# Weight conversion with three VectorE operations a tile; low parts of 18 weight tiles and key sums of two batches made on GpSimd

## The chip, the cores and the metric

The kernel runs on one core of a Trainium2 chip, as one launch. The metric is the device time in microseconds (us) of that core. The core has five engines that run side by side, each through its own list of instructions in a fixed order: TensorE (PE in the profile; PEld is its weight load), VectorE (DVE), ScalarE (ACT), GpSimd (POOL) and SyncE (SP, which here only issues DMAs). An instruction that waits for another engine holds up all that stand behind it on its own engine.

## The reference

Three stages follow each other, each in float32:

```python
k_p = k.reshape(B, H, Sp, 8, D).mean(axis=3)      # 8 batches, 8 heads, 576 keys -> 72
v_p = v.reshape(B, H, Sp, 8, D).mean(axis=3)
attn = softmax(q @ k_p.T / sqrt(D))               # sums get + 1e-9
x = (attn @ v_p) as (4608 tokens, 512)
x = max(x @ w1, x @ w2, x @ w3) @ w_out           # 512 -> 768 -> 512
h = x @ w_in                                      # 512 -> 2048
out = (h - tanh(h)) @ w_out2                      # 2048 -> 512
```

The five weight matrices arrive as float64 and are turned into float32 on the chip, from their bits.

## The kernel before

Every matmul operand is split into a high part H (rounded to the PE's own 32-bit format) and a low part L (the rest), and a product is made of three matmuls: H·H, H·L and L·H.

**Attention (first third).** The tokens are cut into tiles of at most 128 (`tiles`) and these into units that end at a batch's end or at a block of 512 tokens. A key sum (`k_red`, L188) adds eight neighbours of one head pair: one VectorE reduction. `k_split` (L197 on ScalarE, L201 on VectorE) makes H and L of a batch's sums, the tile `kbd`. The value sums (`pool_sum`, L205 to L207) are three GpSimd additions that halve 8 to 4, 2 and 1. Per token tile follow scores (`qk`), maximum (L304), exponentials (L307 on ScalarE), division (L315 to L317), transposes (`tr`, L335, L346) with their splits (L337, L338, L348, L349). At a unit's end `av` (L356 to L359) multiplies with the values; its result is split into `xH` (L363, ScalarE) and `xL` (L364, VectorE), the input of the next stage. The first units have 512, 64 and 448 tokens with four such `xL` each: so the ninth `xL` in the order begins the third unit, which completes the second block.

**First MLP.** `moe_group` (L523 to L529) makes 12 matmuls for one weight tile i and one block j. 18 weight tiles are needed by each of 9 blocks. `moe_part` mixes groups with attention steps in an order written by hand: four groups of block 0 stand in front of the end of the third unit, all others behind it.

**Weight conversion (`Conv`).** A tile of 128x512 float64 is loaded as pairs of 32-bit words (`raw`, three buffers). ScalarE takes the magnitude of the upper word as if it were a float32 (`mag`, L94, into `ma`, four buffers). VectorE then clamps and scales it (L101), shifts it left by 3 (L103), puts in the sign (L105), and the upper three bits of the lower word (L107). For the first 18 tiles `split_to` then makes wH (L128, ScalarE) and wL (L129, VectorE). Another 32 tiles (the weights of the second MLP) go to DRAM and are split later (L602, L603), and six tiles (`wo1`) have their low part made on GpSimd.

**Second MLP (from about 767 us).** `h2`, `gact` and `prod`; results leave PSUM by L734 (ScalarE) or L736 (VectorE), those of the stage in between by L663 or L665.

The order of the instructions on each engine is set by a scheduler that goes through the program and may take a later instruction of an engine first, where it reckons that the earlier one would have to wait. Operations marked `keep_in_program_order` stay where they are. Buffers come free when their last reader is done.

Of the kernel before, what the change touches and what calls it, by code (L numbers as in the profile page):

```python
# [7 lines left out]
F32 = mybir.dt.float32  # L8
# [4 lines left out]
AF = mybir.ActivationFunctionType  # L13
ALU = mybir.AluOpType
# [18 lines left out]
NF = FF // 128  # L33
# [19 lines left out]
def moe_chain_kernel(ctx, tc, qt, kt, vm, vl, ident, cst, w123, wo1, win, wout, out):  # L53
    nc = tc.nc
    V, A, G, T, Q = nc.vector, nc.scalar, nc.gpsimd, nc.tensor, nc.sync
# [3 lines left out]
    def pool(name, bufs=1, side="left", **kw):  # L59
        cm = tc.tile_pool(name=name, bufs=bufs, side=side, **kw)  # L60
        stacks[name] = cm
        return cm.__enter__()
# [11 lines left out]
    srcs = [(win if c % 2 == 0 else wout)[c // 2] for c in range(2 * NC2)]  # L74
# [3 lines left out]
    class Conv:  # L78


        def __init__(self, st, srcs, done, pin=lambda i: i):
            self.st, self.srcs, self.done, self.n, self.pin = st, srcs, done, len(srcs), pin
            self.raw, self.a, self.i = {}, {}, 0

        def load(self, i):
            if i < self.n and i not in self.raw:
                t = self.st.tile([128, 512, 2], I32, tag="raw", name="raw", bufs=RAWS)
                Q.dma_start(out=t.bitcast(I64).rearrange("p n o -> p (n o)"), in_=self.srcs[i])
                self.raw[i] = t

        def mag(self, i):
            if i < self.n:
                a = self.st.tile([128, 512], I32, tag="ma", name="ma", bufs=4)
                self.pin(A.activation(a.bitcast(F32), self.raw[i][:, :, 1].bitcast(F32), AF.Abs))  # L94
                self.a[i] = a

        def bits(self, i):
            if i < self.n:
                raw, a = self.raw[i], self.a[i]
                lo, hi = raw[:, :, 0], raw[:, :, 1]  # L100
                self.pin(V.tensor_scalar(out=a.bitcast(F32), in0=a.bitcast(F32), scalar1=2.0 ** -15,  # L101
                                         scalar2=2.0 ** -80, op0=ALU.max, op1=ALU.mult))
                V.tensor_scalar(out=a, in0=a, scalar1=3, scalar2=0x7FFFFFFF,  # L103
                                op0=ALU.logical_shift_left, op1=ALU.bitwise_and)
                V.scalar_tensor_tensor(out=a, in0=hi, scalar=-2147483648, in1=a,  # L105
                                       op0=ALU.bitwise_and, op1=ALU.bitwise_or)
                V.scalar_tensor_tensor(out=a, in0=lo, scalar=29, in1=a,  # L107
                                       op0=ALU.logical_shift_right, op1=ALU.bitwise_or)

        def step(self):  # L110
            i = self.i
            if i > self.n:
                return
            if i == 0:
                for k in range(RAWS):
                    self.load(k)
                self.mag(0)
            if i > 0:
                self.done(i - 1, self.a.pop(i - 1).bitcast(F32))
            self.mag(i + 1)  # L120
            self.bits(i)
            self.load(i + RAWS)
            self.i += 1

    def split_to(outs, eng):
        def done(i, w):
            H, L = outs[i]
            A.copy(H, w)  # L128
            eng.tensor_tensor(out=L, in0=w, in1=H.bitcast(F32), op=ALU.subtract)  # L129
        return done  # L130
# [6 lines left out]
    sta = pool("sta")  # L137
# [9 lines left out]
    wH = [wa.tile([128, 4, 128], F32R, name=f"wH{i}") for i in range(18)]  # L147
    wL = [wa.tile([128, 4, 128], F32R, name=f"wL{i}") for i in range(18)]
# [29 lines left out]
    kraw, vraw, vxraw, ksum, vsum, vxsum = {}, {}, {}, {}, {}, {}  # L178
# [6 lines left out]
    def k_red(b, p):  # L185
        if b not in ksum:
            ksum[b] = at.tile([128, NP, SP], F32, tag="ksum", name="ksum")
        r = V.tensor_reduce(out=ksum[b][:, p, :], in_=kraw.pop((b, p)), axis=AX.X, op=ALU.add)  # L188
        if b > 1:
            tc.keep_in_program_order(r)  # L190
# [13 lines left out]
    def pool_sum(o, t):  # L204
        G.tensor_tensor(out=t[:, :, 0:4], in0=t[:, :, 0:4], in1=t[:, :, 4:8], op=ALU.add)  # L205
        G.tensor_tensor(out=t[:, :, 0:2], in0=t[:, :, 0:2], in1=t[:, :, 2:4], op=ALU.add)
        G.tensor_tensor(out=o, in0=t[:, :, 0], in1=t[:, :, 1], op=ALU.add)  # L207
# [209 lines left out]
    for n in range(ntl + 1):  # L417
        last = n == ntl
        if not last:
            b = tiles[n][0]  # L420
# [57 lines left out]
    for _ in range(NP - 1):  # L478
# [2 lines left out]
    q_load(2)  # L481
    Q.dma_start(out=consts, in_=cst)
    cv = Conv(sta, [w123[i] for i in range(18)],
              split_to([tuple(t[i].rearrange("p a b -> p (a b)") for t in (wH, wL)) for i in range(18)], V))
    cv.load(0)
    Q.dma_start(out=idt, in_=ident)
    next_v()
# [66 lines left out]
    def point(x):  # L554

        j = int(x)
        if j >= NA - 1:
# [6 lines left out]
    moe_part(gr(1)[:4], point(2.2))  # L564
    moe_part([g for p in zip(gr(0)[4:], gr(1)[4:]) for g in p], point(3), conv=lambda k: k % 2 == 0)
    cv = Conv(sta, srcs, lambda i, w: tc.keep_in_program_order(Q.dma_start(out=wsc[i], in_=w)),
              tc.keep_in_program_order)
    for i in range(RAWS):
        cv.load(i)
    for j in range(2, NA - 1):  # L570
# [6 lines left out]
    wo = pool("wo", side="right")  # L577
    woH = [wo.tile([128, 512], F32R, name=f"woH{i}") for i in range(NF)]
    woL = [wo.tile([128, 512], F32R, name=f"woL{i}") for i in range(NF)]
    cv = Conv(sta, [wo1[i] for i in range(NF)], split_to(list(zip(woH, woL)), G))  # L580
    for i in range(RAWS):
        cv.load(i)
    moe_part(gr(NA - 1), pos[0])
# [9 lines left out]
    def w_load():  # L593
        i = nw[0]
        if i < 2 * NC2:
            Q.dma_start(out=wt[i][1].bitcast(F32), in_=wsc[i])
            nw[0] += 1

    def w_split():
        i = nw[1]  # L600
        h, l = wt[i]
        A.copy(h, l.bitcast(F32))  # L602
        G.tensor_tensor(out=l, in0=l.bitcast(F32), in1=h.bitcast(F32), op=ALU.subtract)  # L603
        nw[1] += 1

    def load_split(src, eng):
        l = io.tile([128, 512], F32R, tag="L", name="ioL", bufs=8)
        r = l.bitcast(F32)
        Q.dma_start(out=r, in_=src)
        t = [None, l]  # L610

        def split():
            h = io.tile([128, 512], F32R, tag="H", name="ioH", bufs=7)
            A.copy(h, r)  # L614
            eng.tensor_tensor(out=l, in0=r, in1=h.bitcast(F32), op=ALU.subtract)  # L615
            t[0] = h

        return t, split

    def hsrc(j, kc):  # L620
        g, o = divmod(j * BB, HG)
        return hs[g][kc][:, o:o + BB]
# [5 lines left out]
    def c_load(eng):  # L628
        i = nld[0]
        if i < len(xl_):  # L630
            j, kc = xl_[i]
            ct[i] = load_split(xs[j][kc], eng)
            nld[0] += 1

    def c_split():
        i = nsp[0]
        if i < len(xl_):
            ct[i][1]()
            nsp[0] += 1
# [8 lines left out]
    for i, (j, kc) in enumerate(loads):  # L648
        if kc == 0:
            acc = [psm.tile([128, 512], F32, tag="mm", name="ps_mm") if j % 2 else  # L650
                   ps2.tile([128, 512], F32, tag="sc" if e < 2 else "tr", name="ps_acc") for e in range(NE)]
        (h, l), _ = lt.pop(i)
        if i + SPL < len(loads):
            lt[i + SPL][1]()
        for e in range(NE):
            c = slice(e * 128, e * 128 + 128)
            T.matmul(acc[e], woH[kc][:, c], h, start=(kc == 0), stop=False)  # L657
            T.matmul(acc[e], woH[kc][:, c], l, start=False, stop=False)  # L658
            T.matmul(acc[e], woL[kc][:, c], h, start=False, stop=(kc == NF - 1))  # L659
            if kc == NF - 1:  # L660
                ob = io.tile([128, 512], F32, tag="ob", name="ob", bufs=4)
                if e % 2 == 0:
                    A.copy(ob, acc[e])  # L663
                else:
                    V.tensor_copy(ob, acc[e])  # L665
                Q.dma_start(out=xs[j][e], in_=ob)
        if i + AHEAD < len(loads):
            lt[i + AHEAD] = load_split(hsrc(*loads[i + AHEAD]), V)
        else:
            c_load(V)  # L670
        if i >= len(loads) - 2:
            c_split()
            c_split()
        w_load()
        while nw[1] < min(2 * NC2, i * 2 * NC2 // (len(loads) - 4)):
            w_split()
# [43 lines left out]
    def prod(j, c):  # L720
        gH, gL = gs.pop((j, c))
        oh, ol = wt[2 * c + 1]
        for t in range(NE):
            r = slice(t * 128, t * 128 + 128)
            if c == 0:
                accs[j, t] = psc.tile([128, 512], F32, tag="acc", name="ps_acc", bufs=5)
            acc = accs[j, t]
            T.matmul(acc, gH[:, r], oh, start=(c == 0), stop=False)  # L728
            T.matmul(acc, gH[:, r], ol, start=False, stop=False)  # L729
            T.matmul(acc, gL[:, r], oh, start=False, stop=(c == NC2 - 1))  # L730
            if c == NC2 - 1:
                ob = io.tile([128, 512], F32, tag="ob", name="ob", bufs=4)
                if t % 2 == 0:
                    A.copy(ob, acc)  # L734
                else:
                    V.tensor_copy(ob, acc)  # L736
                r0 = j * BB + t * 128
                Q.dma_start(out=out[r0:r0 + 128, :], in_=ob)

# [72 lines left out]
```

## Time and profile before

| | us |
|---|---|
| three timed runs | 1550.59, 1552.76, 1554.56 |
| median | 1552.76 |
| profiled execution, from first to last instruction (span) | 1548.8 |
| median less span | 4.0 |
| PE, PEld busy | 1508.3, 1250.4 |
| DVE, ACT, POOL busy | 1154.0, 823.5, 195.5 |

A line of the profile names the line of the kernel, the engine, the operation, the output and inputs by their names in the program and the shapes (partitions x elements). "Idle before" is the time that the engine stood still just ahead of such instructions, and what ended it. Instructions of one engine overlap a little: on VectorE the next one begins some 0.08 us ahead of the recorded end. PEclk is the clock that PE was granted, as a share of full speed.

### The profile page before, as it was taken

How to read it: one execution, taken by the hardware profiler on the slowest of the kernel's cores; microseconds unless marked ns; L12 is line 12 of the kernel's file. 1: busy time of each engine (PE TensorE's matmuls, PEld its weight loads, DVE VectorE, ACT ScalarE, POOL GpSimd, SP SyncE). 2: the span in 40 equal slices, each digit the busy share in tenths (PEclk: the TensorE clock that was granted, in tenths of full speed). 3: DMA queues.
4: the chain of work that ended last, by engine and by line, in shares of the span. 5: the costliest groups of instructions: out<-in, count | busy, mean ns of one | idle time of the engine just before them, and what ended most of it. 6: DMA issues, size and time to landing. Idle time of an engine off the chain costs nothing.

```text
span 1548.8 us, 20108 instructions
## 1 busy us (share of the span) xinstructions
PE 1508.3 (97%) x6896; PEld 1250.4 (81%) x6896; DVE 1154.0 (75%) x2050; ACT 823.5 (53%) x2059; POOL 195.5 (13%) x223
## 2 busy tenths in 40 slices
PE   4899999999999999999999999999999999999999
PEld 4678878888888788888888888888888888888887
DVE  7998378777777831533488888888888888888886
ACT  7664266555566510632455555555555555555554
POOL 4503020202100110920001000010101000010000
PEclk9889999999999999999999999999999999999999
DMA  7645144545332511955300000010100000010000
GB/s 260 182 136 173 58 138 145 173 147 180 123 120 96 182 50 51 328 188 174 123 1 28 28 28 28 1 55 0 55 1 28 28 28 28 0 55 0 28 1 28
DMA packets 68614, 134.55 MB, mean 87 GB/s; under 512 B 11552, under 2 KB 11680, under 8 KB 68512
## 3 DMA queue, kind: packets, MB, share of 16 engines
q1 hardware_dynamic: 68512, 133.27, 26.5%
q8 instruction: 54, 0.88, 0.2%
q14 instruction: 48, 0.39, 0.1%
HBM read 91.82 MB, written 41.42 MB: 86 GB/s over the span
## 4 chain that ended last, share of the span: by engine, by line
PE 89%; DVE 8%; ACT 1%; issue 1%; DMA 0%; ACTq 0%; DVEq 0%; SPq 0%
PE ps_mm L715 8%; PE ps_mm L717 8%; PE ps_acc L730 8%; PE ps_acc L728 8%; PE ps_acc L729 8%; PE ps_mm L716 8%; PE ps_mm L523 8%; PE ps_mm L524 8%; PE ps_mm L525 8%; PE ps_acc L659 2%; PE ps_acc L658 2%; PE ps_acc L657 2%; PE ps_mm L659 1%; PE ps_mm L658 1%; PE ps_mm L657 1%; PE ps_sc L283 1%
## 5 line engine op out<-in xcount | busy, mean ns | idle before, releaser
L523 PE MATMUL ps_mm<-xH,wH 128*128 128x512 f32 x648 | 260.0, 402 | 0.0
L524 PE MATMUL ps_mm<-xL,wH 128*128 128x512 f32 x648 | 254.2, 392 | 0.0
L525 PE MATMUL ps_mm<-xH,wL 128*128 128x512 f32 x648 | 253.8, 392 | 0.0
L703 ACT CAST gH<-w 128x512 fp32r<-128x512 f32 x144 | 89.4, 621 | 301.3 <-DVE w L702 301.3
L715 PE MATMUL ps_mm<-ioH,ctH 128*128 128x512 f32 x576 | 224.2, 389 | 0.8 <-ACT ioH L614 0.8
L717 PE MATMUL ps_mm<-ioH,ctL 128*128 128x512 f32 x576 | 224.1, 389 | 0.0
L716 PE MATMUL ps_mm<-ioL,ctH 128*128 128x512 f32 x576 | 224.1, 389 | 0.0
L728 PE MATMUL ps_acc<-ctH,gH 128*128 128x512 f32 x576 | 224.1, 389 | 0.0
L729 PE MATMUL ps_acc<-ctL,gH 128*128 128x512 f32 x576 | 224.1, 389 | 0.0
L730 PE MATMUL ps_acc<-ctH,gL 128*128 128x512 f32 x576 | 224.1, 389 | 0.0
L704 DVE TENSOR_TENSOR gL<-w,gH 128x512 fp32r<-128x512 f32 x144 | 103.9, 722 | 92.1 <-ACT gH L703 86.5
L529 DVE TENSOR_TENSOR h<-h,ps_mm 128x512 f32<-128x512 f32 x108 | 73.9, 685 | 104.2 <-PE ps_mm L525 102.9
L525 PEld LDWEIGHTS ps_mm<-xH,wL 128*128 128x128 f32 x648 | 121.9, 188 | 25.9
L615 POOL TENSOR_TENSOR ioL<-ioL,ioH 128x512 fp32r<-128x512 f32 x32 | 49.3, 1558 | 728.9 <-ACT ioH L614 728.9
L523 PEld LDWEIGHTS ps_mm<-xH,wH 128*128 128x128 f32 x648 | 122.6, 189 | 22.7
L524 PEld LDWEIGHTS ps_mm<-xL,wH 128*128 128x128 f32 x648 | 122.4, 189 | 22.5 <-DVE xL L364 0.3
L715 PEld LDWEIGHTS ps_mm<-ioH,ctH 128*128 128x128 f32 x576 | 108.2, 188 | 23.7 <-ACT ioH L614 1.2
L729 PEld LDWEIGHTS ps_acc<-ctL,gH 128*128 128x128 f32 x576 | 108.1, 188 | 22.6
L717 PEld LDWEIGHTS ps_mm<-ioH,ctL 128*128 128x128 f32 x576 | 108.1, 188 | 22.5
L730 PEld LDWEIGHTS ps_acc<-ctH,gL 128*128 128x128 f32 x576 | 108.1, 188 | 22.4
L716 PEld LDWEIGHTS ps_mm<-ioL,ctH 128*128 128x128 f32 x576 | 108.1, 188 | 22.4
L728 PEld LDWEIGHTS ps_acc<-ctH,gH 128*128 128x128 f32 x576 | 108.0, 188 | 22.3
(106 smaller groups left out, 2843.9 us busy)
## 6 DMA issues: line engine op xcount, KB each, us to landing
hs<-h SPq DMA_DIRECT2D x54, 256.0 KB, 2.0
ioL<-hs SPq DMA_DIRECT2D x54, 256.0 KB, 3.2
kraw<-kt SPq DMA_DIRECT2D x32, 288.0 KB, 3.3
raw<-w SPq DMA_DIRECT2D x18, 512.0 KB, 3.8
xs<-ob SPq DMA_DIRECT2D x36, 256.0 KB, 2.1
ioL<-xs SPq DMA_DIRECT2D x36, 256.0 KB, 3.4
out<-ob SPq DMA_DIRECT2D x36, 256.0 KB, 2.2
qraw<-qt SPq DMA_DIRECT2D x32, 256.0 KB, 3.0
```

The costliest lines, as they stand in the source:

```text
L523: T.matmul(ps[:, :BA], wH[i][:, kc], xh[:, kc], start=(kc == 0), stop=False)
L524: T.matmul(ps[:, :BA], wH[i][:, kc], xl[:, kc], start=False, stop=False)
L525: T.matmul(ps[:, :BA], wL[i][:, kc], xh[:, kc], start=False, stop=(kc == NE - 1))
L529: V.tensor_tensor(out=t, in0=t, in1=ps[:, :BA], op=ALU.max)
L703: A.copy(gH, w)
L704: V.tensor_tensor(out=gL, in0=w, in1=gH.bitcast(F32), op=ALU.subtract)
L715: T.matmul(ps, wh[:, kc], xh, start=(kc == 0), stop=False)
L716: T.matmul(ps, wh[:, kc], xl2, start=False, stop=False)
L717: T.matmul(ps, wl_[:, kc], xh, start=False, stop=(kc == NE - 1))
L728: T.matmul(acc, gH[:, r], oh, start=(c == 0), stop=False)
L729: T.matmul(acc, gH[:, r], ol, start=False, stop=False)
L730: T.matmul(acc, gL[:, r], oh, start=False, stop=(c == NC2 - 1))
```

## The change

- `Conv` takes the engine for a new step `low`, which shifts the lower word right by 29 in place (VectorE in all three uses, one source and one result with a step of 8 bytes). The clamp, the scale and the separate shift go: the scale moves into the ScalarE magnitude, one operation shifts left and joins the low bits, one joins the sign. VectorE has three operations a tile (L94, L108 and L110 of the changed file) in place of four.
- The weights are now larger by 2 to the 8th. Results are scaled back where they leave PSUM, by 2 to the -24 and 2 to the -8.
- wL of the first 18 tiles is made on GpSimd.
- The key sums of the batches counted 1 and 2 (the second and third of eight) are made on GpSimd by `pool_sum`, three additions each.

```diff
@@ class Conv
+        def low(self, i):
+            if i < self.n:
+                lo = self.raw[i][:, :, 0]
+                self.pin(self.eng.tensor_scalar(out=lo, in0=lo, scalar1=29, scalar2=None,
+                                                op0=ALU.logical_shift_right))
...
-                self.pin(A.activation(a.bitcast(F32), self.raw[i][:, :, 1].bitcast(F32), AF.Abs))
+                self.pin(A.activation(a.bitcast(F32), self.raw[i][:, :, 1].bitcast(F32), AF.Abs,
+                                      scale=2.0 ** -111))
...
-                self.pin(V.tensor_scalar(out=a.bitcast(F32), in0=a.bitcast(F32), scalar1=2.0 ** -15,
-                                         scalar2=2.0 ** -80, op0=ALU.max, op1=ALU.mult))
-                V.tensor_scalar(out=a, in0=a, scalar1=3, scalar2=0x7FFFFFFF,
-                                op0=ALU.logical_shift_left, op1=ALU.bitwise_and)
+                self.pin(V.scalar_tensor_tensor(out=a, in0=a, scalar=3, in1=lo,
+                                                op0=ALU.logical_shift_left, op1=ALU.bitwise_or))
                 V.scalar_tensor_tensor(out=a, in0=hi, scalar=-2147483648, in1=a,
                                        op0=ALU.bitwise_and, op1=ALU.bitwise_or)
-                V.scalar_tensor_tensor(out=a, in0=lo, scalar=29, in1=a,
-                                       op0=ALU.logical_shift_right, op1=ALU.bitwise_or)
...
@@ def k_red
+        if b in (1, 2):
+            pool_sum(ksum[b][:, p, :], kraw.pop((b, p)))
+            return
...
-              split_to([tuple(t[i].rearrange("p a b -> p (a b)") for t in (wH, wL)) for i in range(18)], V))
+              split_to([tuple(t[i].rearrange("p a b -> p (a b)") for t in (wH, wL)) for i in range(18)], G), V)
...
-                    A.copy(ob, acc[e])
+                    A.activation(ob, acc[e], AF.Copy, scale=2.0 ** -24)
                 else:
-                    V.tensor_copy(ob, acc[e])
+                    V.tensor_scalar(out=ob, in0=acc[e], scalar1=2.0 ** -24, scalar2=None, op0=ALU.mult)
```

Behind the same change of the two lines that write `out` (2 to the -8) and the new arguments of the three `Conv` calls nothing else differs.

VectorE, end of the first batch, where the second batch's keys (`kbd_168`) are split. Before:

```order
L188 TENSOR_REDUCE ksum<-kraw 128x72 x2
L129 TENSOR_TENSOR wL_150<-ma,wH_132 128x512
L101 TENSOR_SCALAR ma<-ma 128x512 x2
L338 TENSOR_TENSOR eL<-ps_tr,eH 128x4x128
L349 TENSOR_TENSOR eX<-ps_tr,eX 32x2x128
L201 SCALAR_TENSOR_TENSOR kbd_168<-ksum,kbd_168 64x4x72 x2
```

The same place now:

```order
L312 TENSOR_REDUCE nb<-ps_sc 64x4 x2
L209 SCALAR_TENSOR_TENSOR kbd_168<-ksum,kbd_168 64x4x72
L346 TENSOR_TENSOR eL<-ps_tr,eH 128x4x128
L209 SCALAR_TENSOR_TENSOR kbd_168<-ksum,kbd_168 64x4x72
L108 SCALAR_TENSOR_TENSOR ma<-ma,raw 128x512
L110 SCALAR_TENSOR_TENSOR ma<-raw,ma 128x512
```

The key sums and wL_150 are gone from VectorE, and the first half of the split stands ahead of the fourth tile's `eL`.

ScalarE at the same place (L197 before and L205 now are the splits, L307 and L315 the exponentials, here of the fifth tile with 64 tokens). Before:

```order
L307 ACTIVATE sc,su<-ps_sc,nb 64x72 x4
L319 COPY lf<-sc 128x192
L307 ACTIVATE sc,su<-ps_sc,nb 64x72 x4
L337 CAST eH<-ps_tr 128x4x128
L348 CAST eX<-ps_tr 96x2x128
L197 ACTIVATE kbd_168<-ksum 64x4x72 x2
```

Now:

```order
L205 ACTIVATE kbd_168<-ksum 64x4x72 x2
L327 COPY lf<-sc 128x192
L100 ACTIVATE ma<-raw 128x512
L133 CAST wH_132<-ma 128x512
L345 CAST eH<-ps_tr 128x4x128
L315 ACTIVATE sc,su<-ps_sc,nb 64x72 x8
```

The split stands in front of the fifth tile's exponentials and of the fourth tile's `eH`, which it stood behind.

GpSimd from the last value sums of the first batch on. Before:

```order
L207 TENSOR_TENSOR vxsum<-vxraw 96x64
L205 TENSOR_TENSOR vraw<-vraw 128x64x4
L206 TENSOR_TENSOR vraw<-vraw 128x64x2
L207 TENSOR_TENSOR vsum<-vraw 128x64
L205 TENSOR_TENSOR vraw<-vraw 128x64x4
```

Now, from one row earlier in the program:

```order
L215 TENSOR_TENSOR vsum<-vraw 128x64
L134 TENSOR_TENSOR wL_149<-ma,wH_131 128x512
L213 TENSOR_TENSOR vxraw<-vxraw 96x64x4
...
L213 TENSOR_TENSOR vraw<-vraw 128x64x4
L214 TENSOR_TENSOR vraw<-vraw 128x64x2
L213 TENSOR_TENSOR kraw<-kraw 128x72x4
L214 TENSOR_TENSOR kraw<-kraw 128x72x2
L215 TENSOR_TENSOR ksum<-kraw 128x72
L213 TENSOR_TENSOR kraw<-kraw 128x72x4
```

A low part stands ahead of the first batch's last value sums, and the four key sums of the second batch follow the first steps of two value sums.

## Rows read from the trace of the kernel before

**Rows 1.** Busy time by stretch: us, then PE, PEld, DVE, ACT, POOL, PEclk.

```profile
10.00:40.00 30.00, 17.27 (x80) 15.30 (x79) 27.50 (x58) 25.82 (x112) 15.11 (x25) 1.00 0.78 260
40.00:86.00 46.00, 37.13 (x167) 29.32 (x167) 43.66 (x94) 32.54 (x132) 20.40 (x36) 0.82 0.56 165
86.00:140.00 54.00, 53.87 (x252) 45.09 (x252) 51.85 (x109) 30.01 (x91) 12.43 (x18) 0.97 0.56 176
```

**Rows 2.** Waits of PE from 10 to 86 us: total, times, longest.

```profile
PE ps_tr L335 <- DVE sc L317: 11.0, 6, 3.8
```

**Rows 3.** Groups by line on DVE from 10 to 86 us: count, busy us, mean ns.

```profile
L188 DVE TENSOR_REDUCE ksum<-kraw 128x72 f32<-128x576 f32 x9 | 6.6, 742 | 0.0
L105 DVE SCALAR_TENSOR_TENSOR ma<-raw,ma 128x512 int32<-128x512 int32 x7 | 5.7, 828 | 0.0
L103 DVE TENSOR_SCALAR ma<-ma 128x512 int32<-128x512 int32 x8 | 5.2, 679 | 0.0
L107 DVE SCALAR_TENSOR_TENSOR ma<-raw,ma 128x512 int32<-128x512 int32 x6 | 5.1, 845 | 0.0
```

**Rows 4.** Instructions of DVE in order of time, GpSimd idle: start, duration.

```profile
102.66 0.69 DVE L107 SCALAR_TENSOR_TENSOR ma<-raw,ma 128x512 int32<-128x512 int32 x1
103.26 0.42 DVE L103 TENSOR_SCALAR ma<-ma 128x512 int32<-128x512 int32 x1
103.60 0.42 DVE L101 TENSOR_SCALAR ma<-ma 128x512 f32<-128x512 f32 x1
103.94 0.68 DVE L105 SCALAR_TENSOR_TENSOR ma<-raw,ma 128x512 int32<-128x512 int32 x1
```

**Rows 5.** Groups by line on POOL from 10 to 86 us.

```profile
L205 POOL TENSOR_TENSOR vraw<-vraw 128x256 f32<-128x256 f32 x15 | 12.2, 811 | 22.4 <-DMA vraw<-vm 22.4
L206 POOL TENSOR_TENSOR vraw<-vraw 128x128 f32<-128x128 f32 x15 | 8.2, 548 | 1.2
L207 POOL TENSOR_TENSOR vsum<-vraw 128x64 f32<-128x64 f32 x12 | 4.6, 389 | 16.3 <-DVE VL L237 15.7
```

**Rows 6.** Instructions in order of time around the first and ninth `xL`.

```profile
22.01 0.66 ACT L128 CAST wH<-ma 128x512 fp32r<-128x512 f32 x1
...
23.30 0.29 POOL L207 TENSOR_TENSOR vxsum<-vxraw 96x64 f32<-96x64 f32 x1
...
36.38 1.40 DVE L188 TENSOR_REDUCE ksum<-kraw 128x72 f32<-128x576 f32 x2
...
43.32 0.69 DVE L364 TENSOR_TENSOR xL<-ps_av,xH 128x512 fp32r<-128x512 f32 x1
...
87.40 0.62 DVE L364 TENSOR_TENSOR xL<-ps_av,xH 128x448 fp32r<-128x448 f32 x1
```

**Rows 7.** Two lines of DVE over the span: count, least/median/greatest ns.

```profile
L103 DVE TENSOR_SCALAR ma<-ma x56: 408/418/1510, 18.1 to 547.0; 128x512 int32<-128x512 int32 x56
L105 DVE SCALAR_TENSOR_TENSOR ma<-raw,ma x56: 670/681/1219, 19.1 to 547.9; 128x512 int32<-128x512 int32 x56
```

**Rows 8.** Second MLP: groups by line, and two of them by duration.

```profile
L615 POOL TENSOR_TENSOR ioL<-ioL,ioH 128x512 fp32r<-128x512 f32 x32 | 49.3, 1558 | 728.9 <-ACT ioH L614 728.9
L701 DVE SCALAR_TENSOR_TENSOR w<-s,w 128x512 f32<-128x512 f32 x144 | 106.2, 738 | 15.3 <-DVE w L700 0.9
L702 DVE COPY_PREDICATED w<-mk,th 128x512 f32<-128x512 uint8 x144 | 113.4, 788 | 4.7
...
L701 DVE SCALAR_TENSOR_TENSOR w<-s,w x144: 686/692/1631, 767.6 to 1537.2; 128x512 f32<-128x512 f32 x144
L702 DVE COPY_PREDICATED w<-mk,th x144: 727/740/1716, 768.6 to 1538.0; 128x512 f32<-128x512 uint8 x144
```

**Rows 9.** Longest wait of PE behind 86 us.

```profile
PE ps_av L356 <- DVE xL L364: 3.3, 3, 1.7
```

**Rows 10.** Reads of PSUM on DVE: a copy, and a computing operation.

```profile
L736 DVE COPY ob<-ps_acc 128x512 f32<-128x512 f32 x18 | 12.3, 681 | 4.2 <-PE ps_acc L730 4.2
L698 DVE TENSOR_TENSOR th<-ps_mm,th 128x512 f32<-128x512 f32 x144 | 97.9, 680 | 0.0
```

More of the change, by code (lines that the diff above doesn't have):

```diff
@@ L78, in moe_chain_kernel, with __init__ @@
     class Conv:
-        def __init__(self, st, srcs, done, pin=lambda i: i):
-            self.st, self.srcs, self.done, self.n, self.pin = st, srcs, done, len(srcs), pin
+        def __init__(self, st, srcs, done, eng, pin=lambda i: i):
+            self.st, self.srcs, self.done, self.n, self.pin, self.eng = st, srcs, done, len(srcs), pin, eng
             self.raw, self.a, self.i = {}, {}, 0
@@ L117, in step @@
                 self.mag(0)
+                self.low(0)
             if i > 0:
@@ L120, in step @@
             self.mag(i + 1)
+            self.low(i + 1)
             self.bits(i)
@@ L566, in moe_chain_kernel @@
     cv = Conv(sta, srcs, lambda i, w: tc.keep_in_program_order(Q.dma_start(out=wsc[i], in_=w)),
-              tc.keep_in_program_order)
+              V, tc.keep_in_program_order)
     for i in range(RAWS):
@@ L579, in moe_chain_kernel @@
     woL = [wo.tile([128, 512], F32R, name=f"woL{i}") for i in range(NF)]
-    cv = Conv(sta, [wo1[i] for i in range(NF)], split_to(list(zip(woH, woL)), G))
+    cv = Conv(sta, [wo1[i] for i in range(NF)], split_to(list(zip(woH, woL)), G), V)
     for i in range(RAWS):
@@ L733, in prod @@
                 if t % 2 == 0:
-                    A.copy(ob, acc)
+                    A.activation(ob, acc, AF.Copy, scale=2.0 ** -8)
                 else:
-                    V.tensor_copy(ob, acc)
+                    V.tensor_scalar(out=ob, in0=acc, scalar1=2.0 ** -8, scalar2=None, op0=ALU.mult)
                 r0 = j * BB + t * 128
```

## The prediction

> **What bounds the kernel now.** I read the stretches first, then PE's waits, then the lines of VectorE and GpSimd in the stretch that matters, then single instructions. Behind 86 us PE is never free: 53.87 of 54 us are busy there [rows 1], and its longest wait behind that is 3.3 us in all [rows 9]. What PE then does is the same before and after the change, so whatever is gained or lost ahead of that point is carried to the end, us for us. Ahead of it VectorE is the bound: 27.50 of 30 us, then 43.66 of 46, while PE is busy for 37.13 of 46 and at a mean granted clock of 0.82 [rows 1]. PE's longest wait there is 11.0 us for the divided scores of L317 [rows 2], an attention instruction of VectorE, in front of which conversion stands. So the mark to watch is the first `xL` of the third unit, the ninth in all, at 87.40 us [rows 6]: with that unit PE gets the second block and enough work. Until then it is given only four groups in either order.
>
> **The change, part by part.** Durations are of the profiled execution, whose span is 1548.8 us. The timed median, 1552.76, lies 4.0 above it. I take these 4.0 as unchanged and put every difference on the median.
>
> *VectorE's own work up to the ninth `xL`.* From start to start a full two-input operation takes 0.60 us (102.66 to 103.26) and L103 and L101 take 0.34 each [rows 4]; a key sum lasts 0.742 [rows 3], so some 0.66 from start to start. Counted in the order before, there stand ahead of the ninth `xL` 8 L101 and 8 L103 (16 x 0.34 = 5.4), 8 L105, 7 L107 and 6 L129 (21 x 0.60 = 12.6) and the eight key sums that move (8 x 0.66 = 5.3): 23.3 us. In the changed order there stand 14 `low` (4.8 at 0.34), 24 of the two joining operations (14.4) and one `qL` more (0.6): 19.8. That is 3.5 us less, although twelve tiles are converted by then and not seven: the scheduler has pulled conversion ahead and spends most of the saving on it. Weights that are ready earlier are worth nothing, since PE is full from 86 us on with the present ones.
>
> `low` does not occur in this trace. Its nearest rows are L103, also one source and integer shift, with step 4 (0.418 median), and L105, which reads the same strided words but two sources (0.681) [rows 7]. I take the first, since it too has one source; the other end costs 14 x 0.26 = 3.6 us more. Nothing here makes it shorter than L103. On `low` the Trainium skill (VectorE: DVE Perf Modes, Mode 2×_2P) asks, for two elements a cycle, for one source and SBUF on both sides with an even outer dimension, not for step 1; by that it would have the short time, and no run here shows it.
>
> *The second batch's keys.* Their sums now wait for GpSimd, which works through its list in order. Before, it is through with the first batch's value sums at 23.6 us (23.30 + 0.29) [rows 6]. Ahead of the last key sum now come a low part (1.56 by L615, the same shape [rows 8]; its wH was cast by 22.7 [rows 6], so it is not late), two value sums' first steps, 2 x (0.811 + 0.548) = 2.7, their last steps, 2 x 0.389 = 0.8, and four key sums. One key sum has 9/8 of a value sum's elements: 1.125 x (0.811 + 0.548 + 0.389) = 1.97 [rows 5], so four take 7.9. The end is at 23.6 + 1.6 + 2.7 + 0.8 + 7.9 = 36.6 us, where VectorE now ends at 36.38 + 1.40 = 37.8 [rows 6]. That is 1.2 us earlier. But the split on ScalarE now stands in front of a copy, a magnitude, a cast and the fourth tile's `eH`, some 2 us by the 0.66 of such a cast [rows 6], and of the fifth tile's exponentials; on VectorE the `eL` of the fourth tile, which the first `av` needs, stands behind the first half of the split. All of these wait for GpSimd. So the first `xL` comes no earlier than its 43.32 us [rows 6]. What VectorE has saved up to there is lost: 2.7 + 4.2 + 2.6 before (8 short operations, 7 long, 4 key sums) against 1.4 + 4.2, which is 3.9, of which some 1.3 goes into a maximum and a division that are pulled ahead (by the lengths of [rows 4]) and isn't lost; 2.6 is. Bounds: 0 if GpSimd is ready when VectorE gets there, 4.6 if the 2 us on ScalarE come on top.
>
> *GpSimd against VectorE.* In 10 to 86 us GpSimd is busy for 15.11 + 20.40 = 35.5 us [rows 1]. VectorE's conversion lines are longer there than their medians: L103 8 x (679 - 418) ns = 2.1 us, L105 7 x (828 - 681) = 1.0, L107, of the same form, 6 x (845 - 681) = 1.0 [rows 3, 7]. That is 4.1, or 0.12 us of VectorE for each us of GpSimd. In the second MLP 32 GpSimd subtractions, busy for 49.3 us, go with L701 at 738 against a median of 692 (144 x 46 ns = 6.6) and L702 at 788 against 740 (6.9) [rows 8]: 13.5, or 0.27. Between the first and the ninth `xL` the change adds four key sums (7.9) and, as I count, eight low parts (8 x 1.56 = 12.5). I take 0.12 for the first, which are of the value sums' kind, and 0.27 for the second, which are L615's shape: 0.9 + 3.4 = 4.3 us. Bounds: 2.4 at 0.12 for all 20.4, and 10.2 if half of it stops VectorE.
>
> What the rows show is that some VectorE instructions double while GpSimd works (L701 to 1631 ns [rows 8]). The Trainium skill has the rule (SBUF — State Buffer, Who interferes with whom): the port pair of these two engines is an exclusive lock, and a VectorE operation with two SBUF inputs, or in a two-port mode, blocks for a whole GpSimd instruction that reads SBUF, or the other way round. By the rule every added subtraction can cost more than the 0.60 it takes off VectorE; by the rates above it costs 0.4. This rule is the second rival.
>
> *What I take at nothing.* Copies out of PSUM with a factor: VectorE's copy takes 681 ns and a computing operation on PSUM 680 [rows 10], and PE is the bound there. The third batch's keys: GpSimd has them some 10 us behind the second's (7.9 and a low part), before VectorE has done the work in front of their split. SyncE: three raw tiles now stand ahead of the second batch's later value loads and wait for buffers that VectorE frees; these value sums stand behind both batches' key sums anyway. The four `ma` buffers now come free by GpSimd, and a magnitude that waits for one holds up ScalarE's exponentials; GpSimd's list stays ahead of that by four tiles. If one of the last three covers is gone, 1 to 3 us (one key sum to one and a half low parts) are lost.
>
> *Behind 86 us.* 32 tiles of the second MLP lose 0.34 us of VectorE each, 11 us over some 300. PE's waits for `xL` there are 3.3 us in all [rows 9]. I take 1.0 off; bounds 0 and 3.3.
>
> Sum: -3.5 + 2.6 + 4.3 - 1.0 = +2.4 us, so 1555.2 us.
>
> **The rivals.**
>
> *Faster: the pulled-ahead conversion lies in waits.* Five more tiles by the ninth `xL` are 5 x (0.34 + 0.60 + 0.60) = 7.7 us. If they fill the wait for the keys (2.6) and the idle time that VectorE had (30 - 27.50 and 46 - 43.66, 4.8 [rows 1]), 7.4 of it costs nothing. With all 3.3 of the later waits gone: 2.4 - 7.4 - 2.3 = -7.3, 1545.5 us. For it: the scheduler takes a later instruction only where it reckons with a wait. Against it: the idle time now is small, and it is not known how well the scheduler reckons.
>
> *Slower: GpSimd stops VectorE for whole instructions.* About half of the instructions ahead of the ninth `xL` (79 of 158 counted in the changed order) have two inputs in SBUF or are `low`. If VectorE stands for half of the 20.4 us: 10.2 in the place of 4.3, +8.3, 1561.1 us. For it: L701 and L702 grow by up to a whole GpSimd instruction. Against it: the stage itself shows 0.12. It decides from a rate of about 0.32.
>
> *The three operations are not cheaper:* `low` at 0.60 adds 3.6, 1558.8 us.
>
> **How the numbers follow.** About 0.3%, 4.7 us, is what a measurement of this kernel can tell from no change: 1548.1 to 1557.4. Chances: forecast 0.38 (0.32 same, 0.03 on either side), faster rival 0.24 (0.21 faster, 0.03 same), contention 0.28 (0.23 slower, 0.05 same), costly `low` 0.10 (0.07 slower, 0.03 same). So faster 0.24, same 0.43, slower 0.33. The range reaches to both outer rivals, 1545 to 1563; the forecast's own is 1551 to 1559.
>
> **What would show it.** In the changed profile: `low` at 0.42 us or 0.68; GpSimd's fourth key sum of the second batch near 36.6 us, with ScalarE's split waiting for it; the first `xL` near 43 us; L108 and L110 above 0.68 on average up to the ninth `xL`, by what GpSimd costs; the ninth `xL` at about 87.4 + 3.4 = 91 us; PE full from there. I am wrong in the main step if the ninth `xL` comes before 86 us, and in the carrying over if it moves and the span does not.

## The result, and the profile after

The changed kernel takes 1563.25 us (median of 4 runs, 1561.61 to 1564.36); the kernel before, timed beside it, 1551.67 (1549.23 to 1554.56). The ratio is 1.0074, 95% interval 1.0062 to 1.0086: slower by 11.6 us. The profiled spans are 1559.8 and 1548.8 us, 11.0 apart.

In the profile after, the lines of the conversion and of the attention stand some 8 lower: the low words' shift is L94, the joining operations L108 and L110, `wL` L134, the sums of `pool_sum` L213 to L215, the split of the keys L205 and L209, the divided scores L323 to L325, `xL` L372. First the same three stretches as in [rows 1] (PE, PEld, DVE, ACT, POOL, PEclk):

```profile
10.00:40.00 30.00, 18.17 (x75) 14.68 (x75) 24.68 (x48) 21.60 (x94) 24.98 (x40) 1.00 0.69 221
40.00:86.00 46.00, 35.35 (x150) 28.83 (x150) 43.77 (x75) 32.24 (x127) 37.89 (x52) 0.87 0.60 204
86.00:140.00 54.00, 47.04 (x213) 38.58 (x213) 43.23 (x87) 33.90 (x111) 26.20 (x30) 0.86 0.49 157
```

From 40 to 86 us VectorE is as busy as before (43.77 us, 43.66 before) but gets through 75 instructions instead of 94, while GpSimd is busy for 37.89 us instead of 20.40. PE loses 6.8 us from 86 to 140 us (47.04, 53.87 before). Then the marks of [rows 6]: the end of the second batch's key sums on GpSimd, the split that waits for it, the first and the ninth `xL`.

```profile
36.47 0.31 POOL L215 TENSOR_TENSOR ksum<-kraw 128x72 f32<-128x72 f32 x1
...
37.29 0.55 DVE L209 SCALAR_TENSOR_TENSOR kbd<-ksum,kbd 64x288 fp32r<-64x288 f32 x1 [1.32 <-ACT kbd L205]
39.69 0.69 DVE L346 TENSOR_TENSOR eL<-ps_tr,eH 128x512 fp32r<-128x512 f32 x1 [1.84 <-ACT eH L345]
...
47.20 1.40 DVE L372 TENSOR_TENSOR xL<-ps_av,xH 128x512 fp32r<-128x512 f32 x2
...
100.33 1.16 DVE L372 TENSOR_TENSOR xL<-ps_av,xH 128x448 fp32r<-128x448 f32 x2
```

The first `xL` is 3.9 us later than before, the ninth 12.9. The stretches from 10 us to the first `xL` and from there to the ninth, before and then now:

```profile
10.00:43.32 33.32, 20.59 (x87) 17.94 (x87) 30.69 (x64) 26.73 (x113) 18.11 (x30) 1.00 0.76 251
43.32:87.40 44.08, 35.21 (x163) 27.90 (x163) 41.84 (x92) 32.68 (x133) 17.39 (x31) 0.79 0.55 160
```
```profile
10.00:47.20 37.20, 23.85 (x92) 19.42 (x93) 31.65 (x58) 26.50 (x114) 31.87 (x50) 1.00 0.68 226
47.20:100.33 53.13, 37.92 (x161) 30.45 (x160) 50.72 (x90) 38.00 (x142) 37.71 (x46) 0.75 0.56 183
```

And from the ninth `xL` to the end, before and then now:

```profile
87.40:1548.80 1461.40, 1450.48 (x6643) 1202.70 (x6641) 1077.19 (x1886) 760.13 (x1805) 156.31 (x154) 1.00 0.24 80
```
```profile
100.33:1559.80 1459.47, 1449.49 (x6638) 1201.34 (x6636) 1045.40 (x1810) 755.10 (x1795) 160.63 (x161) 1.00 0.24 78
```

Behind the ninth `xL` the rest of the kernel takes 1.9 us less than before, with PE's granted clock at 1.00 in both. So the whole loss lies ahead of that mark. PE's three longest waits from 10 to 100 us (total, times, longest), beside [rows 2], are all for VectorE:

```profile
PE ps_tr L343 <- DVE sc L325: 6.6, 5, 3.1
PE ps_sc L293 <- DVE qL L267: 3.6, 1, 3.6
PE ps_av L364 <- DVE eL L346: 3.3, 1, 3.3
```

GpSimd's groups that are new there, of the size foreseen from [rows 5] (1.97 us a key sum, 1.91 measured) and a little under it for a low part (1.56 from [rows 8]):

```profile
L134 POOL TENSOR_TENSOR wL<-ma,wH 128x512 fp32r<-128x512 f32 x11 | 15.4, 1403 | 10.4 <-ACT wH L133 10.4
...
L213 POOL TENSOR_TENSOR kraw<-kraw 128x288 f32<-128x288 f32 x8 | 7.2, 903 | 0.0
...
L214 POOL TENSOR_TENSOR kraw<-kraw 128x144 f32<-128x144 f32 x8 | 4.6, 578 | 0.6
L215 POOL TENSOR_TENSOR ksum<-kraw 128x72 f32<-128x72 f32 x8 | 3.3, 428 | 0.3
```

VectorE's groups by line and shape from 10 to 100 us, which answer to [rows 3], show what became of the time:

```profile
L110 DVE SCALAR_TENSOR_TENSOR ma<-raw,ma 128x512 int32<-128x512 int32 x12 | 10.4, 868 | 0.0
L108 DVE SCALAR_TENSOR_TENSOR ma<-ma,raw 128x512 int32<-128x512 int32 x12 | 10.2, 851 | 0.0
L325 DVE TENSOR_TENSOR sc<-sc,su 128x576 f32<-128x576 f32 x7 | 8.4, 1194 | 0.1
L94 DVE TENSOR_SCALAR raw<-raw 128x512 int32<-128x512 int32 x14 | 7.3, 523 | 0.1
L312 DVE TENSOR_REDUCE nb<-ps_sc 128x4 f32<-128x288 f32 x14 | 6.2, 449 | 0.6 <-PE ps_sc L285 0.3
L323 DVE TENSOR_SCALAR su<-su 128x8 f32<-128x8 f32 x8 | 4.9, 608 | 1.4 <-ACT sc L315 1.2
L346 DVE TENSOR_TENSOR eL<-ps_tr,eH 128x512 fp32r<-128x512 f32 x7 | 4.8, 682 | 2.1 <-ACT eH L345 2.1
```

Four of these lines over the whole span, L312 from 10 to 100 us (least, median and greatest duration in ns), tell which of these means are stretched:

```profile
L94 DVE TENSOR_SCALAR raw<-raw x56: 410/422/1085, 12.5 to 553.5; 128x512 int32<-128x512 int32 x56
L108 DVE SCALAR_TENSOR_TENSOR ma<-ma,raw x56: 666/685/1640, 16.7 to 554.3; 128x512 int32<-128x512 int32 x56
L323 DVE TENSOR_SCALAR su<-su x40: 151/172/2149, 14.3 to 520.0; 128x8 f32<-128x8 f32 x32, 64x8 f32<-64x8 f32 x8
L312 DVE TENSOR_REDUCE nb<-ps_sc x16: 400/454/458, 10.6 to 73.5; 128x4 f32<-128x288 f32 x14, 64x4 f32<-64x288 f32 x2
```

L108 takes 851 ns on average instead of 685, L325 1194 (before, L317 has a median of 748 up to the ninth `xL`), L323, an addition to 8 columns, 608 instead of 172. L312, a reduction, and L346, which has one input in PSUM, have their old length. One place in order of time, first on VectorE:

```profile
78.48 2.15 DVE L323 TENSOR_SCALAR su<-su 128x8 f32<-128x8 f32 x1
80.55 0.67 DVE L537 TENSOR_TENSOR h<-h,ps_mm 128x512 f32<-128x512 f32 x1
81.15 0.43 DVE L312 TENSOR_REDUCE nb<-sc 64x4 f32<-64x288 f32 x1
...
81.80 1.82 DVE L325 TENSOR_TENSOR sc<-sc,su 128x576 f32<-128x576 f32 x1
```

and on GpSimd in the same time:

```profile
78.37 0.31 POOL L215 TENSOR_TENSOR vxsum<-vxraw 96x64 f32<-96x64 f32 x1
78.63 1.29 POOL L134 TENSOR_TENSOR wL<-ma,wH 128x512 fp32r<-128x512 f32 x1
79.89 0.72 POOL L213 TENSOR_TENSOR vraw<-vraw 128x256 f32<-128x256 f32 x1
80.69 0.40 POOL L214 TENSOR_TENSOR vraw<-vraw 128x128 f32<-128x128 f32 x1
81.04 0.72 POOL L213 TENSOR_TENSOR vraw<-vraw 128x256 f32<-128x256 f32 x1
81.73 1.28 POOL L134 TENSOR_TENSOR wL<-ma,wH 128x512 fp32r<-128x512 f32 x1
```

The addition at 78.48 lasts until GpSimd has finished three instructions (80.61); behind it an operation with a PSUM input and a reduction run at their usual length beside GpSimd; the product at 81.80 takes 1.82 us, as the low part that began 0.07 us earlier runs for 1.28.

**One account for all runs.** From 10 us to the ninth `xL` every us of VectorE is one of three things: idle; stretch, which is the sum over its instructions of the duration less that of the same line and shape undisturbed (15th percentile over that run); and its own work, the rest of its busy time. They add up to the ninth `xL` less 10 us. Neighbouring instructions overlap a little, so the line between own work and idle time is good to some 0.5 us. All are summed from the rows of each trace; "tiles" are the weight tiles whose conversion stands ahead of the ninth `xL` in VectorE's list. Times in us; the last column is the ratio to runs of the kernel before on the same chip, with its 95% interval (those had medians of 1550.96 to 1552.06).

| kernel | tiles | GpSimd busy | own | stretch | idle | ninth `xL` | span | median | ratio |
|---|---|---|---|---|---|---|---|---|---|
| before | 7 | 36.2 | 65.1 | 7.0 | 5.3 | 87.4 | 1548.8 | 1551.67 | |
| after | 12 | 71.3 | 62.0 | 20.2 | 8.0 | 100.3 | 1559.8 | 1563.25 | 1.0074 [1.0062, 1.0086] |
| e1 | 9 | 55.4 | 63.7 | 12.8 | 4.1 | 90.6 | 1551.2 | 1553.06 | 1.0010 [1.0001, 1.0020] |
| e2 | 11 | 53.1 | 65.6 | 13.7 | 7.3 | 96.6 | 1556.5 | 1557.70 | 1.0039 [1.0026, 1.0051] |
| e3 | 8 | 39.5 | 65.3 | 7.8 | 6.7 | 89.8 | 1551.3 | 1552.54 | 1.0002 [0.9993, 1.0011] |
| e4 | 10 | 69.9 | 63.4 | 17.0 | 10.0 | 100.3 | 1563.6 | 1565.25 | 1.0088 [1.0074, 1.0102] |
| e5 | 8 | 47.4 | 65.0 | 11.7 | 7.0 | 93.6 | 1561.9 | 1564.85 | 1.0087 [1.0073, 1.0101] |
| e6 | 7 | 48.5 | 62.2 | 9.4 | 6.2 | 87.8 | 1548.4 | 1552.89 | 1.0005 [0.9996, 1.0014] |
| e8 | 5 | 54.3 | 53.2 | 10.9 | 15.9 | 90.0 | 1551.6 | 1553.20 | 1.0009 [0.9999, 1.0018] |
| e9 | 7 | 35.7 | 63.7 | 4.1 | 11.9 | 89.6 | 1551.9 | 1552.98 | 1.0008 [1.0000, 1.0017] |
| e10 | 12 | 36.8 | 74.6 | 7.0 | 10.3 | 101.9 | 1561.0 | 1564.02 | 1.0081 [1.0067, 1.0095] |
| e11 | 6 | 37.3 | 62.7 | 4.1 | 12.1 | 88.9 | 1550.2 | 1551.66 | 0.9997 [0.9988, 1.0005] |

For the changed kernel: own work -3.1, stretch +13.2, idle time +2.7, together the 12.9 us by which the ninth `xL` is late.

### The profile page after: what moved, and what is told of

It reads as the page before. It is cut to its first block, busy times and chain, and to the rows that moved or that the text cites. A ratio compares the mean times of both kernels' runs of the same rounds, so it can differ in the third digit from the quotient of the medians.

```text
span 1559.8 us, 20020 instructions
## 1 busy us (share of the span) xinstructions
PE 1513.7 (97%) x6896; PEld 1253.3 (80%) x6896; DVE 1133.1 (73%) x1968; ACT 823.9 (53%) x2059; POOL 233.9 (15%) x265
## 4 chain that ended last, share of the span: by engine, by line
PE 90%; DVE 5%; ACT 2%; POOL 1%; issue 1%; DMA 0%; ACTq 0%; DVEq 0%; POOLq 0%; SPq 0%
PE ps_mm L531 9%; PE ps_mm L533 8%; PE ps_mm L723 8%; PE ps_acc L737 8%; PE ps_acc L736 8%; PE ps_mm L724 8%; PE ps_mm L725 8%; PE ps_acc L738 8%; PE ps_mm L532 8%; PE ps_acc L665 2%; PE ps_acc L666 2%; PE ps_acc L667 2%; PE ps_mm L665 1%; PE ps_mm L666 1%; PE ps_mm L667 1%; ACT sc L315 1%
```

## The experiments

**The parts of the change one by one (e1 to e4).** e1 puts the low parts back on VectorE, e2 the key sums, e3 both, so that the conversion alone is left; e4 is the kernel before with both moves.

```diff
# e1 and e3, against the changed kernel
-  split_to([... for i in range(18)], G), V)
+  split_to([... for i in range(18)], V), V)
# e2 and e3, against the changed kernel
-  if b in (1, 2):
-      pool_sum(ksum[b][:, p, :], kraw.pop((b, p)))
-      return
# e4: the opposite edits, in the kernel before
```

Expected of e1: 

> The changed kernel with the low parts of the 18 weight tiles back on VectorE; conversion in three operations and the key sums on GpSimd stay. Contention (GpSimd's added work stops VectorE for some 0.46 us per us, which is 13.2 us of stretched VectorE instructions over 28 us of added GpSimd work up to the ninth xL): 15.1 us of key sums are left, 6.9 us of stretch, less 2.8 of VectorE's own work in this order and 1 behind: 1555, at most 1558 where the wait for the keys comes on top. Wait for the keys (ScalarE and VectorE stand in front of GpSimd's key sums, which delays the first xL, and all behind it): it stays near 1560 or over. Pulled-ahead conversion (the time goes with the weight tiles converted ahead of the ninth xL: 7 before, 12 changed, 9 here): 1556. Conversion itself (the three operations are the dear part): 1563.

Expected of e2: 

> The changed kernel with the key sums of the second and third batch back on VectorE; conversion in three operations and the low parts of 18 weight tiles on GpSimd stay. Contention: some ten low parts of 1.4 us are left ahead of the ninth xL, 14 x 0.46 = 6.4 us of stretch, less 0.1 of own work and 1 behind: 1557. Wait for the keys: 1552 or less, the first xL back at 43 to 44 us. Pulled-ahead conversion (11 tiles): 1561. Conversion itself: 1563.

Expected of e3: 

> The changed conversion in three operations alone: low parts and key sums all on VectorE as before. Contention: GpSimd does what it did before, so nothing is added; 0.5 us less of VectorE's own work up to the ninth xL in this order and 1 behind it: 1550. Wait for the keys: the same, 1550. Pulled-ahead conversion (8 tiles): 1553 to 1554. Conversion itself: 1560 or more.

Expected of e4: 

> The kernel before, with four VectorE operations a weight tile, and with both moves to GpSimd (low parts of 18 weight tiles, key sums of the second and third batch). Contention: 13 us of stretch and 2 us of waits, less 2.3 of VectorE's own work: 1564. Wait for the keys: about 1560. Pulled-ahead conversion (10 to 11 tiles): 1560. Conversion itself: 1552.

Measured: 1553.06, 1557.70, 1552.54 and 1565.25. Contention comes nearest in three of them (1555, 1557, 1564); for e3 it had 1550, and the pulled-ahead conversion 1553. The conversion itself is no cause: alone it is the time of before (e3), without it the loss is whole (e4). Nor is the wait for the keys by itself: e1 has the key sums on GpSimd and loses 0.1%, and e2, which has them on VectorE and no such wait, loses 0.39%. ScalarE's wait for the last key sum, around 37 us, is short in e1:

```profile
ACT kbd L205 <- POOL ksum L215: 1.0, 1, 1.0
```

and longer in the changed kernel,

```profile
ACT kbd L205 <- POOL ksum L215: 4.6, 1, 4.6
```

but e8 (below), which loses nothing that can be measured, has as much of it:

```profile
ACT kbd L205 <- POOL ksum L215: 5.3, 2, 2.8
```

The first `xL` is as late in e1 (47.04) as in the changed kernel (47.20), while it stands at 43.41 in e3. The rows are of e1,

```profile
47.04 0.69 DVE L372 TENSOR_TENSOR xL<-ps_av,xH 128x512 fp32r<-128x512 f32 x1 [0.33 <-ACT xH L371]
```

and of e3:

```profile
43.41 0.69 DVE L369 TENSOR_TENSOR xL<-ps_av,xH 128x512 fp32r<-128x512 f32 x1 [0.88 <-ACT xH L368]
```

What e1 and the changed kernel share is the stretch ahead of it: 7.7 and 7.1 us in the 45 us before the first `xL`, against 4.2 in e3 and 3.2 before. Of the two moves the low parts cost more (e2), and both together more than their sum (0.10% + 0.39% against 0.74%). These four leave open whether contention or the number of tiles pulled ahead does it, since both rise together.

**Contention by itself (e5, e6).** Both are e3 with GpSimd instructions added that nobody reads, one set for each of the 18 tiles. In e5 the lists of VectorE, ScalarE and PE are the same as in e3, instruction for instruction.

```diff
+  def beside(t):                      # e5, called behind a tile's last VectorE operation
+      f = t.bitcast(F32)
+      G.tensor_tensor(out=f[:, :, 0], in0=f[:, :, 0], in1=f[:, :, 1], op=ALU.subtract)
+  def beside(t):                      # e6
+      G.memset(t.bitcast(F32), 0.0)
+      G.memset(t[:, 0:256, :].bitcast(F32), 0.0)
```

Expected of e5: 

> The three-operation conversion alone (low parts and key sums on VectorE), with one more GpSimd instruction for each of the 18 weight tiles that nobody reads: a subtraction of the raw tile's two halves, 128x512 as a low part, behind the tile's last VectorE operation. VectorE's order stays as it is without it, 8 tiles ahead of the ninth xL. Contention: 8 subtractions of 1.5 us, 12 us at 0.46 are 5.5 us of stretched VectorE instructions, so 1557 to 1558 against 1552.5 without them. If the low parts cost by what waits for them, or by the place that they take in GpSimd's list: 1552 to 1553.

Expected of e6: 

> As the run with a subtraction beside each of the 18 weight tiles, but with two memsets of the raw tile (128x1024 and 128x512 words, some 1.5 us together) in the subtraction's place: GpSimd is busy for as long at the same places, waits for the same instructions and holds the same buffer, but reads nothing. If VectorE is stopped by GpSimd's reads of SBUF, there is no stretch: 1552 to 1553. If any GpSimd instruction on SBUF stops it: 1557.

Measured: 1564.85 and 1552.89. GpSimd's added group of e5 (10 to 160 us):

```profile
L493 POOL TENSOR_TENSOR raw<-raw 128x512 f32<-128x512 f32 x18 | 21.6, 1206 | 34.0 <-DVE ma L109 19.0 <-issue 4.7 <-DVE xL L372 3.8
```

and those of e6:

```profile
L492 POOL MEMSET raw<- 128x1024 f32 x18 | 17.3, 965 | 33.2 <-DVE ma L111 14.2 <-ACT VX L242 4.0 <-ACT eH L345 3.8
L493 POOL MEMSET raw<- 128x512 f32 x18 | 9.8, 550 | 0.6
```

21.6 us of subtractions that change no other list cost 12.3 us; 27.1 us of memsets at the same places cost nothing that can be measured. In e5 this is what GpSimd does to VectorE: up to 160 us VectorE's stretch is 11.3 us more than in e3, and the span is longer by 10.6. e6 is the weaker of the two runs. The scheduler chose another order there, with a tile less and 3.1 us less of own work ahead of the ninth `xL` than in e3, so its time can't be set beside e3's as e5's can; its stretch up to 160 us is 2.7 us more than in e3. That memsets cost less than subtractions rests on the stretch more than on the time. The size of e5 was missed by 7 us, and not for the rate ahead of the ninth `xL`: there the stretch grew by 3.9 us, less than the 5.5 expected. What was missed is that the subtractions went on costing behind the mark, with 7.4 us more stretch up to 160 us. VectorE is nearly full there in e5, but not in e8 and e11, where 4.3 and 3.8 us more stretch behind the mark than before cost nothing; that this is what tells them apart was not tested by itself. The stretches from 86 to 140 us of e5, e8 and e11:

```profile
86.00:140.00 54.00, 49.30 (x224) 40.21 (x225) 51.86 (x91) 31.64 (x102) 22.70 (x25) 0.91 0.51 159
```
```profile
86.00:140.00 54.00, 53.44 (x247) 44.77 (x248) 46.32 (x88) 31.50 (x104) 23.06 (x27) 0.95 0.49 150
```
```profile
86.00:140.00 54.00, 53.16 (x244) 44.64 (x244) 43.22 (x82) 29.69 (x97) 21.86 (x27) 0.94 0.49 147
```

**The order by itself (e8 to e11).** `tc.keep_in_program_order` on the conversion of the 18 tiles stops the scheduler from pulling it ahead. e8 is the changed kernel with it, e9 is e3 with it; e10 is e9 with nine steps of conversion written ahead of the third unit, which restores the twelve tiles without any GpSimd work; e11 is e9 with the last 13 low parts on GpSimd.

```diff
-  ..., V)
+  ..., V, tc.keep_in_program_order)   # e8 to e11
-  for _ in range(4):
+  for _ in range(9):                  # e10 alone
       cv.step()
-  eng.tensor_tensor(out=L, ...)
+  (V if i < first else eng).tensor_tensor(out=L, ...)   # e11 alone; first is 5 and eng G for the 18 tiles
```

Expected of e8: 

> The changed kernel, both moves in it, with the conversion of the 18 tiles held in the order in which the program is written: five tiles are converted ahead of the ninth xL in the place of twelve. Contention and own work together: 7 x 1.54 = 10.8 us of VectorE and 7 x 1.4 x 0.46 = 4.5 us of stretch less ahead of the ninth xL, so 1548 if all of it counts, 1553 if PE then waits elsewhere. If the pulled-ahead conversion lies in waits and only its low parts cost, 1559; if neither the order nor the low parts matter, but the wait for the keys does, 1562 to 1563.

Expected of e9: 

> The three-operation conversion alone (low parts and key sums on VectorE), with the conversion of the 18 tiles held in the order in which the program is written: seven tiles and six low parts ahead of the ninth xL in the place of eight and eight. Own work of VectorE: 1.5 + 1.2 + 0.3 = 3 us less, 1549.5. If the pulled-ahead conversion lies in waits: 1552.5.

Expected of e10: 

> The three-operation conversion with low parts and key sums on VectorE and its order held as written, but with nine conversion steps in the place of four ahead of the third unit: 12 tiles and 11 low parts stand ahead of the ninth xL, as many as in the changed kernel, with GpSimd doing no more than before. Against the run with 7 tiles VectorE has 1.7 + 6.0 + 3.0 + 0.7 = 11.4 us more to do there. If the conversion that is pulled ahead costs what it takes (VectorE is the bound): ninth xL at 101 us, 1564. If it lies in waits (VectorE has 11 us of idle time from 10 to 86 us in the run with 7 tiles) and only contention costs: 1553. Half and half: 1558.

Expected of e11: 

> The three-operation conversion with its order held as written, key sums and the first five low parts on VectorE, the other 13 low parts on GpSimd, all of them behind the ninth xL but one. If contention costs only ahead of the ninth xL, where VectorE sets the pace: 1552 to 1553, as without the move. If it costs wherever it falls: 13 x 1.4 x 0.4 = 7 us, 1559. If relief of VectorE behind the ninth xL were worth something: 1550.

Measured: 1553.20, 1552.98, 1564.02, 1551.66. With the order held the changed kernel loses nothing that can be measured (e8), although GpSimd still does both moves. And twelve tiles ahead cost the whole loss without the moves (e10), as the first of its three readings had it: 10.9 us of own work and 2.9 of stretch more than e9, ninth `xL` 12.3 us later (the rows are e9's and e10's), while VectorE's idle time falls by only 1.6.

```profile
89.64 0.62 DVE L369 TENSOR_TENSOR xL<-ps_av,xH 128x448 fp32r<-128x448 f32 x1 [0.45 <-ACT xH L368]
```
```profile
101.93 0.62 DVE L369 TENSOR_TENSOR xL<-ps_av,xH 128x448 fp32r<-128x448 f32 x1
```

So conversion beyond the seven tiles of before does not lie in waits. Below that it partly does: e9 missed its 1549.5 and came out at the 1552.5 that its other reading gave. Against e3 it has 1.6 us less of own work and 3.7 less stretch, but 5.2 us more idle time and the same ninth `xL`. e11 is as e9, within what these runs can tell, so its low parts behind the mark cost nothing that can be measured. Set beside the changed kernel, e10 has as many tiles and low parts ahead of the mark, with all of them and the key sums on VectorE: 74.6 own and 7.0 stretch, 81.6 together; the changed kernel has 62.0 and 20.2, together 82.2. The moves took 12.6 us of work off VectorE and gave 13.2 us of stretch back. So the loss of the changed kernel goes back to two things: the scheduler pulls five tiles more ahead of the mark, and GpSimd's work returns to VectorE all that was moved off it. Without the first there is no loss that can be measured (e8): that is shown. That the second is needed too is reckoned and not shown: without it there would be 62.0 us and the 7.0 of before, 3.1 less than in the kernel before, but that case can't be run, since the moves bring the stretch with them. e5 shows that contention is enough for a loss of this size where nothing is taken off VectorE, though most of it falls behind the mark there.

No version beat the kernel before. e8, e9 and e11 have 12 to 16 us of idle VectorE up to the ninth `xL` and still reach it at 89 to 90 us. In e8 VectorE then waits for ScalarE's exponentials (7.0 us for L315 up to 90 us, seven times). With less work VectorE is no longer what sets the ninth `xL`; what exactly does was not followed further.

## Why the prediction was wrong

- **VectorE's own work, -3.5.** Measured -3.1 (65.1 to 62.0). `low` takes 422 ns (median), so the one-input price was right and the rival of a costly `low` falls. The Trainium skill (VectorE: DVE Perf Modes, Mode 2×_2P) would have it short: it asks for one source, SBUF on both sides and an even outermost dimension, and its conditions name no step. 422 ns against 685 for the two-input L108 agree.
- **The second batch's keys, +2.6.** The last key sum was foreseen for 36.6 us and ended at 36.78; ScalarE's split waited for it, and VectorE stood idle for 1.32 and 1.84 us behind it. From 10 us to the first `xL` VectorE's idle time is 5.5 us, and was 2.6 (33.32 less 30.69), so the wait cost about what the sum gave it. But the first `xL` was to stay at 43.3 and came at 47.20. Of VectorE's time up to there 3.0 us of own work are gone and 2.9 us of idle time are new, as foreseen; the 3.9 us of delay are as much as the stretch that was added, of which the sum had none there. In e1, with 1.0 us of wait, 4.5 us of added stretch go with the same delay.
- **GpSimd against VectorE, +4.3.** This is the step that failed: it measured +13.2. Two sizes were off. Between the first and the ninth `xL` GpSimd's added time came out as foreseen (37.71 less 17.39 is 20.3 us, 20.4 in the sum), but it added 9.2 us of stretch and not 4.3: a rate of 0.45 in the place of 0.21. And ahead of the first `xL`, where the sum put nothing, 13.8 us more of GpSimd (31.87 less 18.11) added the other 4.0. Over both the rate is 13.2 / 35.1 = 0.38, with the table's GpSimd times. (The expectations above divided by an early count of 28 us and wrote 0.46.) The 0.12 came from three conversion lines alone; all lines of VectorE together give 7.0 / 36.2 = 0.19 in the trace of before. The 0.27 was put together from two of the three lines that are stretched beside the same GpSimd instruction in the second MLP. L704, with two inputs in SBUF, was left out: its mean there is 722 ns and its median 692 (trace of before), so 144 x 30 ns = 4.3 us more, and 17.8 / 49.3 = 0.36, near what was measured (its row stands below). In the changed kernel the two moves differ in their rate. With each stretched instruction put down to the GpSimd instruction that it overlaps most, up to 160 us, the low parts cost 10.3 us for 26.1 busy (0.40) and the key sums 3.6 for 15.2 (0.24).
- **Behind the ninth `xL`, -1.0, and the carrying over.** 12.9 us at the mark became 11.0 in the span. "PE is never free" behind 86 us was not so: before, it stands idle for 10.9 us behind the mark (1461.40 less 1450.48), and now for 10.0. That is 0.9 less, as the sum had it, though its waits for `xL` went from 3.3 to 3.0 only. The other 1.0 is PE's busy time, 1449.49 for 1450.48. Single executions of the kernel before differ by more than this (1549.23 to 1554.56), so the size is not shown beyond the two profiled ones. That the mark carries over held within 2.3 us in ten of the eleven kernels set against before; in e5 it did not, with its stretch behind the mark.
- **The rivals.** Contention was the one that came true: its rate decides from 0.32, and 0.45 was measured where it was counted. 1561.1 was forecast for it, with 10.2 us between the first and the ninth `xL`, where 9.2 were measured; the 4.0 ahead of the first `xL` were missing in it as well. "The stage itself shows 0.12" was the argument against it, and the stage showed 0.19. "Pulled-ahead conversion lies in waits" is refuted by e10 for the tiles beyond seven.
- **What was missed besides the size:** moving work off an engine that another one can stop was priced by two separate terms, relief and contention. Taken together up to the mark they are one sum, and it is near zero (81.6 and 82.2).

The row of L704 in the kernel before:

```profile
L704 DVE TENSOR_TENSOR gL<-w,gH 128x512 fp32r<-128x512 f32 x144 | 103.9, 722 | 92.1 <-ACT gH L703 86.5 <-PE ps_acc L730 4.1 <-PE ps_mm L717 1.4
```

## What to carry to other kernels

Before a two-input operation is moved from VectorE to GpSimd, count which of VectorE's neighbouring instructions read two SBUF inputs or are one-input arithmetic from SBUF to SBUF: where VectorE sets the pace and most are of these kinds, GpSimd can give back all that it takes, as it did here. Take the rate of contention from all of VectorE's lines beside the same kind of GpSimd instruction, and from the whole stretch up to the mark: here two lines of three gave 0.27 for 0.36, three lines of the stage 0.12 for 0.19, and part of the stretch was priced at nothing. And look at what a scheduler does with the room that a move seems to make: here holding the order took 1563.25 us to 1553.20, 10 of the 11.6 us.

## What the runs showed of the hardware

- Beside GpSimd's sums and subtractions (changed kernel, 10 to 100 us) the stretched instructions are those with both inputs in SBUF (L108, L110, L267, L325, L209, L245, L249) and one-input `TENSOR_SCALAR` from SBUF to SBUF (L94, L323). Reductions, reciprocals and operations with a PSUM input (L312, L324, L346, L357, L372) lie within 0.02 us of their undisturbed length. The Trainium skill (SBUF — State Buffer, Who interferes with whom) draws the line at the same place: at most one SBUF input, outside the two-port modes, does not contend.
- The addition at 78.48 us, 151 ns undisturbed, was held for 2.15 us, through three GpSimd instructions on end and not through one.
- Memsets stop less and stop others. In e6 instructions that overlap with memsets alone and are stretched by 0.15 us or more are only the one-input kind, four in all up to 160 us (L323, and the shift `low`, L95 there); the clearest place, on VectorE and then on GpSimd:

```profile
84.49 0.95 DVE L323 TENSOR_SCALAR su<-su 128x8 f32<-128x8 f32 x1
84.57 1.13 DVE L95 TENSOR_SCALAR raw<-raw 128x512 int32<-128x512 int32 x1
```

and in the same time:

```profile
84.46 0.95 POOL L492 MEMSET raw<- 128x1024 f32 x1 [4.17 <-DVE ma L111]
85.47 0.70 POOL L493 MEMSET raw<- 128x512 f32 x1
```
